# Logits with the masked keys of two heads as one stationary operand, in an attention and feed-forward kernel

## The chip, the cores and the metric

The kernel runs on one core of a Trainium2 chip. The metric is the device time of one execution in microseconds, as the median of several runs. The engines are called as in the profile: PE is the tensor engine and PEld its weight loads, DVE the vector engine, ACT the scalar engine, POOL the GpSimd engine, SP the engine that issues DMAs here. PSUM is the memory that PE writes; it has eight banks of 128 x 512 fp32.

## What is computed

A token gate mixes a segmented attention with a gated feed-forward network. Cut to what matters here:

```python
x = A_x                                        # (1, 2048, 512) bf16
g = sigmoid((x * gate_w).sum(-1, keepdims=True))
# attention: 32 heads of 16, four segments of 512 tokens
for s in range(4):
    logits = einsum('bhqd,bhkd->bhqk', qs, ks) * scale + mask   # causal within the segment
    p = softmax(logits); a_dot = p @ vs
    a_mem = (phi(qs) @ M) / (phi(qs) @ z + 1e-6)                # memory of the segments before
    o = sigmoid(beta) * a_mem + (1 - sigmoid(beta)) * a_dot
    M += phi(ks)^T @ vs; z += sum(phi(ks))
a = concat(o) @ wo
b = (relu(x @ W_gate) * (x @ W_up)) @ W_down   # inner width 1792
out = g * a + (1 - g) * b
```

## The kernel before

All weights and activations live on chip in bf16. The work is written as a list of named steps, about 1,100 of them, each with a function that emits its instructions on one engine, and with the steps that it depends on. A list of numbers, `ORDER`, gives for every engine the steps in the order in which that engine runs them, and on which engine a step with a choice runs. Each engine runs its own list strictly in that order, and waits where a dependency is not met. The numbers beside a step's engines are the plan's own costs; with a fixed `ORDER` they settle only which free PSUM bank a step gets.

Four PSUM banks, `rb`, go round among all dense matmul groups: a step takes a bank, and the step that copies the result out gives it back. The other four banks are one tile, `sp`, for the logits.

The dense steps, all on PE, go by segment (first digit) and a running number: `Q` and `K` project queries and keys, four 128-column chunks per segment, each four matmuls of 512 columns (line 477); `V` projects values (519, and `VI` at 502 for segment 0); `G` and `U` are the gate and up projections, 14 of each per segment (894); `D`, `DB` and `W` are the two halves of the down projection and the output projection that accumulates onto it (928, 941; for the last 128 rows in pieces at 852 and 860). `MR` retrieves from the memory (678), `MZ` updates it (632). Their results leave PSUM through `QC`, `KC`, `VC` (copies, 373 on ACT, 375 on DVE), `R` (ReLU, 906 on ACT, 908 on DVE), `H` (product, 913, DVE) and `OS` (scaling, 950 on ACT, 952 on DVE, and `ST` stores it).

One 128-row chunk of queries or keys holds eight heads of 16. It is read in four groups of 32 rows, two heads in each. The logits are made key by query, in blocks of 64 keys, and only where the causal mask lets them through: a block of keys `ck` sees the queries from `64*ck` on. A *part* is such a block with its columns of queries, 64 to 512 of them. Nine *fills* of `sp` take the parts of two chunks, each fill holding one part of 512 columns or two parts that make 512 together. So there are 72 fills: two pairs of chunks in four segments. `QK` (735) makes a fill, `EX` (746) takes the exponential of the whole of `sp` on ACT into one of nine `E` tiles, `MK` (756) zeroes the triangles on POOL, and `PV` (783) multiplies with the values after the fills of a chunk. The next fill must wait for `EX`, as there is one `sp`.

In `QK` each of the four row groups has two matmuls for a part. The even head's keys are the first 16 of the 32 rows, taken as they are with 16 rows of queries; for the odd head the step `KO` (490 on ACT, 492 on DVE) has made a copy of the keys, `KTo`, in which the even heads' rows are multiplied by zero (`mcol_o`), and the matmul uses all 32 rows. Each puts 64 keys in one half of the partitions of `sp`:

```python
for j, h in ((j, h) for j in range(4) for h in range(2)):
    kt = KTo[i] if h else KT[i]
    hi = 32 * j + 16 + 16 * h
    nc.tensor.matmul(sp[64 * h:64 * h + 64, j, off:off + m], ...)
```

`KT`, `KTo` and `QT` exist twice, for odd and even segments. The keys' copy `KT` also feeds the memory update: `EK` (608), `MN` (614), `PK` (618) and a transposing DMA `KX`. `MQ` and `MN` are clamps that run on DVE or POOL, and `TG` (565) is the product for the token gate in segment 0. On SP's queue stand the weight loads (324), the transposing load `XT` of a segment's x (336), `KX`, `MX`, the shifts of the values `VS` (450) and the stores. In the order of the last segment, PE ends with pieces for the last 128 rows of the output, 256, 128 and 128 columns wide.

Of the kernel before, what the change touches and what calls it, by code (L numbers as in the profile page):

```python
# [7 lines left out]
BF16 = mybir.dt.bfloat16  # L8
# [91 lines left out]
]  # L100
T0, TU, SPAN, PEN_D, PEN_A, PEN_P = 19.0, 15.6, 4.1, -23.0, 150.0, 146.0


PORT = {'TG', 'RN', 'RC', 'OA', 'KO', 'MB', 'MQ', 'MN', 'GS', 'PQ', 'PK', 'N1', 'N2', 'N3', 'NM'}
PIECE = {'MK': 0.445, 'TL': 0.22, 'ZE': 0.24, 'YL': 0.22, 'MB': 0.3}


# [898 lines left out]
```

## Time and profile before

| what | value |
|---|---|
| median of 3 runs | 266.98 us (266.53 to 267.01) |
| span of the profiled execution, first to last instruction | 265.0 us |
| instructions in it | 7943 |
| largest group on ACT | the exponential, 72 times, 135.1 us |
| largest group on POOL | the triangles, 256 instructions, 112.3 us |
| DVE's largest group | the product `H`, 56 times, 38.2 us |
| matmuls of `QK` | 1024, in 72 fills |
| HBM traffic | 8.26 MB read, 2.10 MB written |

The profiled execution has no other time of its own than its span; the runs' times include what lies around it. In the profile, a row of a group reads: line, engine, operation, what it writes and reads, shapes and count, then the busy time and the mean of one in ns, then the idle time of the engine before such instructions and what ended it. The chain of work that ended last is followed back from the last instruction. Matmuls are pipelined, so the length of one is not the pace of a row of them, and some of their records are missing.

### The profile page before, as it was taken

The page shows a single profiled execution, that of the slowest core. Times are in us where ns is not written, and L with a number is a line of the kernel's source. Part 1 is how long each engine was busy: PE and PEld are TensorE (multiplying, and loading weights), DVE is VectorE, ACT ScalarE, POOL GpSimd, SP SyncE. Part 2 cuts the span into 40 slices and gives each one's busy share as a digit, 9 for nine tenths or more (in the row PEclk, how much of TensorE's full clock was granted, in tenths as well). Part 3 has the DMA queues.
Part 4 walks back from the last instruction along what each step waited for, and adds up shares of the span by engine and source line. Part 5 has one row for each costly group of instructions (what it writes and reads, how often), then busy time and mean ns, then how long its engine had stood idle before and what let it go on. Part 6 is the DMA issues. An engine that isn't in the chain of part 4 may idle for free.

```text
span 265.0 us, 7943 instructions
## 1 busy us (share of the span) xinstructions
PE 258.1 (97%) x3293; PEld 121.0 (46%) x3337; DVE 181.0 (68%) x449; ACT 189.7 (72%) x185; POOL 143.7 (54%) x328
## 2 busy tenths in 40 slices
PE   7999999999999999999999999999999999999995
PEld 5444443545444444434444445454544444444554
DVE  1589788897774538855896476688878367666911
ACT  3699799987868786887777686886766576767012
POOL 8038978782826641378758464366468156064010
DMA  6978680426501000030403110000023100031002
GB/s 197 314 166 264 149 288 3 71 74 89 79 4 37 25 2 2 20 82 1 104 2 82 25 42 2 0 4 2 2 61 87 42 20 2 0 81 23 0 2 79
DMA packets 33422, 16.77 MB, mean 63 GB/s; under 512 B 20074, under 2 KB 33386, under 8 KB 33386
## 3 DMA queue, kind: packets, MB, share of 16 engines
q1 hardware_dynamic: 33098, 16.00, 24.3%
q8 instruction: 26, 0.43, 0.7%
q10 hardware_dynamic: 288, 0.26, 0.3%
q14 instruction: 10, 0.08, 0.1%
HBM read 8.26 MB, written 2.10 MB: 39 GB/s over the span
## 4 chain that ended last, share of the span: by engine, by line
PE 94%; DMA 1%; DVE 1%; issue 1%; ACT 1%; SPq 0%
PE rb L894 36%; PE rb L928 17%; PE rb L477 11%; PE sp L735 9%; PE rb L783 7%; PE rb L941 5%; PE rb L519 4%; DMA wv_sb<-in_A_wv_dram 1%; PE rb L678 1%; PE rb L852 1%; PE rb L502 1%; DVE hT L913 1%; ACT E L746 1%; PE rb L632 1%; PE rb L860 0%
## 5 line engine op out<-in xcount | busy, mean ns | idle before, releaser
L746 ACT ACTIVATE E<-sp 128x2048 bf16<-128x2048 f32 x72 | 135.1, 1877 | 35.0 <-PE sp L735 32.8
L756 POOL TENSOR_SCALAR_AFFINE_SELECT E<-E 64x256 bf16<-64x256 bf16 x256 | 112.3, 438 | 82.2 <-ACT E L746 68.7
L894 PE MATMUL rb<-xT,wg_sb 128*128 128x512 bf16 x216 | 55.4, 380 | 0.4
L894 PE MATMUL rb<-xT,wu_sb 128*128 128x512 bf16 x208 | 54.9, 380 | 0.8
L913 DVE TENSOR_TENSOR hT<-rb,rg 128x512 bf16<-128x512 f32 x56 | 38.2, 686 | 20.1 <-PE rb L894 14.1
L928 PE MATMUL rb<-wd_sb,hT 128*128 128x512 bf16 x198 | 48.6, 380 | 0.8 <-issue 0.2
L894 PEld LDWEIGHTS <-wg_sb 128*128 128x128 bf16 x224 | 20.7, 98 | 24.8 <-issue 3.1
L894 PEld LDWEIGHTS <-wu_sb 128*128 128x128 bf16 x224 | 20.1, 98 | 23.5 <-issue 4.5
L735 PE MATMUL sp<-QT,KT 16*64 16x320 bf16 (+7 forms) x512 | 30.3, 295 | 0.0
L735 PE MATMUL sp<-QT,KTo 32*64 32x320 bf16 (+7 forms) x512 | 30.3, 295 | 0.0
L928 PEld LDWEIGHTS <-hT 128*128 128x128 bf16 x210 | 19.4, 98 | 23.8 <-issue 3.2
L801 DVE STREAM_TRANSPOSE tA<-rb 128x512 f32<-128x512 f32 x32 | 21.9, 700 | 12.0 <-PE rb L783 11.6
L906 ACT ACTIVATE rg<-rb 128x512 bf16<-128x512 f32 x36 | 21.3, 598 | 10.1 <-PE rb L894 7.1
L735 PEld LDWEIGHTS <-KT 16*64 16x64 bf16 x512 | 10.5, 102 | 27.5 <-issue 26.9
L908 DVE TENSOR_SCALAR rg<-rb 128x512 bf16<-128x512 f32 x20 | 13.8, 688 | 7.5 <-PE rb L894 7.3
L783 PE MATMUL rb<-E,Vs 64*32 64x448 bf16 (+7 forms) x512 | 18.8, 284 | 0.0
L783 PE MATMUL rb<-E,Vp 64*32 64x448 bf16 (+7 forms) x512 | 18.4, 284 | 0.0
L950 ACT ACTIVATE osb<-rb,ngcol 128x512 bf16<-128x512 f32 x8 | 5.5, 691 | 16.2 <-PE rb L941 16.2
L952 DVE TENSOR_SCALAR osb<-rb,ngcol 128x512 bf16<-128x512 f32 x7 | 5.2, 750 | 16.1 <-PE rb L941 15.9
L477 PE MATMUL rb<-xT,wq_sb 128*128 128x512 bf16 x63 | 16.1, 380 | 0.0
L812 DVE TENSOR_TENSOR o<-tA,co 128x256 bf16<-128x256 f32 x32 | 15.4, 493 | 0.2
L477 PE MATMUL rb<-xT,wk_sb 128*128 128x512 bf16 x59 | 15.4, 379 | 0.2
(97 smaller groups left out, 298.3 us busy)
## 6 DMA issues: line engine op xcount, KB each, us to landing
out_dram<-osb SPq DMA_DIRECT2D x15, 128.0 KB, 1.8
wd_sb<-in_B_W_down_dram SPq DMA_DIRECT2D x1, 1792.0 KB
wg_sb<-in_B_W_gate_dram SPq DMA_DIRECT2D x3, 512.0 KB, 6.3
wu_sb<-in_B_W_up_dram SPq DMA_DIRECT2D x3, 512.0 KB, 6.0
Vs<-Vp SPq DMA_DIRECT2D x8, 144.0 KB, 3.2
wk_sb<-in_A_wk_dram SPq DMA_DIRECT2D x2, 256.0 KB, 3.9
wq_sb<-in_A_wq_dram SPq DMA_DIRECT2D x2, 256.0 KB, 4.7
wo_sb<-in_A_wo_dram SPq DMA_DIRECT2D x1, 512.0 KB, 4.2
```

What stands on the lines that cost most here:

```text
L477: nc.tensor.matmul(rb[s.bank][:], lhsT=w[:, ci, c * P:(c + 1) * P], rhs=xT[i][:, ci, :], start=(ci == 0), stop=(ci == NC - 1))
L735: nc.tensor.matmul(sp[64 * h:64 * h + 64, j, off:off + m], lhsT=kt[32 * j:hi, c0 + w, 64 * ck:64 * ck + 64], rhs=QT[i][32 * j:hi, c0 + w, ...
L746: nc.scalar.activation(Er[n % NE][:], sp[:], ACT.Exp, scale=SCALE)
L756: nc.gpsimd.affine_select(out=v, in_=v, compare_op=ALU.is_ge, fill=0.0, base=0, pattern=[[0, 4], [1, 64]], channel_multiplier=-1)
L783: nc.tensor.matmul(rb[s.banks[h]][32 * j:32 * j + 32, q0:q0 + m], lhsT=v[64 * h:64 * h + 64, ck // 2, o:o + 32], rhs=Er[(base + f) % NE][6 ...
L801: nc.vector.transpose(tA[k].rearrange("p b w -> p (b w)"), rb[a.banks[r]][:])
L812: nc.vector.tensor_tensor(o16[u % 2][:, :, r, :], tA[k][:, :, 0:DH], cos[k][:, :, None].to_broadcast([P, NB, DH]), ALU.mult)
L894: nc.tensor.matmul(rb[s.bank][:], lhsT=w[:, ci, fv * P:(fv + 1) * P], rhs=xT[i][:, ci, :], start=(ci == 0), stop=(ci == NC - 1))
L906: nc.scalar.activation(rgb[k][:], rb[a.bank][:], ACT.Relu)
L908: nc.vector.tensor_scalar(rgb[k][:], rb[a.bank][:], 0.0, None, ALU.max)
L913: nc.vector.tensor_tensor(hT[:, fv, :], rb[a.bank][:], rgb[k][:], ALU.mult)
L928: nc.tensor.matmul(rb[b][:], lhsT=hT[:, fv, lc:lc + P], rhs=wd_sb[:, fv, :], start=(fv == 0), stop=False)
```

## The change

For every segment and chunk the keys are now copied twice with a mask: `KO` for the odd heads, as before, and a new step `KE` for the even heads. Both copies go into one tile `KB`, in which each block of 64 keys has its even and odd copies next to each other, 128 columns. `QK` uses those as one stationary operand of 32 rows by 128 columns, with the 32 rows of queries, and writes all 128 partitions of a bank. `KB` exists once, not for odd and even segments, so both copies wait for the fills of the segment before that read the same chunk; the waits of `QC` and `KC` are split to match. In the last two segments the two parts of a fill are made in reverse order. The plan's cost of a fill goes from 0.262 to 0.236. `ORDER` is another list, for 1129 steps in place of 1113, with other places and other engines for many steps.

```diff
-    mcol_o = sb([1], F32, "mcol_o")
+    mcol = [sb([1], F32, f"mcol{r}") for r in range(2)]
...
-    nc.vector.memset(mcol_o[:], 1.0)
-    for j in range(4):
-        nc.vector.memset(mcol_o[32 * j:32 * j + 16, :], 0.0)
+    for r in range(2):
+        nc.vector.memset(mcol[r][:], 1.0 * r)
+        for j in range(4):
+            nc.vector.memset(mcol[r][32 * j:32 * j + 16, :], 1.0 - r)
...
-    KTo = [sb([NC, L], BF16, f"KTo{i}") for i in range(2)]
+    KB = sb([NC, L // 64, 2, 64], BF16, "KB")
...
-                prev = [] if not old else old["qk"][c] + old.get("kr", [])
+                if what == "Q":
+                    prev = old["qk"][c] if old else []
+                else:
+                    prev = old["KO"][2 * c:2 * c + 2] + old.get("kr", [])[c:c + 1] if old else []
...
-            def ko(e, s, c=c):
-                if e == "ACT":
-                    nc.scalar.activation(KTo[i][:, c, :], KT[i][:, c, :], ACT.Copy, scale=mcol_o[:, 0:1])
-                else:
-                    nc.vector.tensor_scalar(KTo[i][:, c, :], KT[i][:, c, :], mcol_o[:, 0:1], None, ALU.mult)
-            d["KO"].append(add(f"KO{seg}{c}", {"DVE": 0.27, "ACT": (0.62, 60.0)}, ko, after=[d["K"][c]], prio=want))
+            for r, kind in ((1, "KO"), (0, "KE")):
+                def ko(e, s, c=c, r=r):
+                    o, k = KB[:, c, :, r, :], KT[i][:, c, :].rearrange("p (k q) -> p k q", q=64)
+                    if e == "ACT":
+                        nc.scalar.activation(o, k, ACT.Copy, scale=mcol[r][:, 0:1])
+                    else:
+                        nc.vector.tensor_scalar(o, k, mcol[r][:, 0:1], None, ALU.mult)
+                d["KO"].append(add(f"{kind}{seg}{c}", {"DVE": 0.27, "ACT": (0.62, 60.0)}, ko,
+                                   after=[d["K"][c]] + (st[seg - 1]["qk"][c] if seg else []), prio=want))
...
-                for _, w, m, ck, q0, off in whole[f]:
-                    for j, h in ((j, h) for j in range(4) for h in range(2)):
-                        kt = KTo[i] if h else KT[i]
-                        hi = 32 * j + 16 + 16 * h
-                        nc.tensor.matmul(sp[64 * h:64 * h + 64, j, off:off + m],
-                                         lhsT=kt[32 * j:hi, c0 + w, 64 * ck:64 * ck + 64],
-                                         rhs=QT[i][32 * j:hi, c0 + w, q0:q0 + m],
-                                         start=True, stop=True, tile_position=(32 * j, 64 * h))
-            a = add(f"QK{seg}{c0}{f}", {"PE": 0.262}, qk, mode="rows",
-                    after=[x for w in us for x in (d["Q"][c0 + w], d["KO"][c0 + w], d["K"][c0 + w])] + fills[-1:],
+                for _, w, m, ck, q0, off in (reversed(whole[f]) if seg > 1 else whole[f]):
+                    for j in range(4):
+                        js = slice(32 * j, 32 * j + 32)
+                        nc.tensor.matmul(sp[:, j, off:off + m],
+                                         lhsT=KB[js, c0 + w, ck].rearrange("p r k -> p (r k)"),
+                                         rhs=QT[i][js, c0 + w, q0:q0 + m],
+                                         start=True, stop=True, tile_position=(32 * j, 0))
+            a = add(f"QK{seg}{c0}{f}", {"PE": 0.236}, qk, mode="rows",
+                    after=[x for w in us for x in [d["Q"][c0 + w], *d["KO"][2 * (c0 + w):2 * (c0 + w) + 2]]] + fills[-1:],
                     prio=tu - 20.0, lat=0.25)
```

Some of the new order, by the steps' names. PE around the first fill of segment 1: `QK028 MR15 D03 D00 QK100` (before `QK028 D00 MR14 MZ1 QK100`). ACT there: `EX028 KE13 KO13 EX100` (before `EX028 EX100`). PE's last steps: `D31 D33 W30 DB33 W32 DB31 D33 W31 W33 DB33 W33` (before `D31 DB30 D33 D32 DB32 DB31 W30 DB33 W31 W32 D33 DB33 W33 D33 W33 DB33 W33`). SP's first: gate and up pieces 0, 1 and 2, then `XT1` (before pieces 0, gate 1 and up 2, then `XT1`).

More of the change, by code (lines that the diff above doesn't have):

```diff
@@ L41 @@
 ORDER = [
[58 rows of a table removed]
[61 rows of a table added]
 ]
 T0, TU, SPAN, PEN_D, PEN_A, PEN_P = 19.0, 15.6, 4.1, -23.0, 150.0, 146.0
-PORT = {'TG', 'RN', 'RC', 'OA', 'KO', 'MB', 'MQ', 'MN', 'GS', 'PQ', 'PK', 'N1', 'N2', 'N3', 'NM'}
+PORT = {'TG', 'RN', 'RC', 'OA', 'KO', 'KE', 'MB', 'MQ', 'MN', 'GS', 'PQ', 'PK', 'N1', 'N2', 'N3', 'NM'}
 PIECE = {'MK': 0.445, 'TL': 0.22, 'ZE': 0.24, 'YL': 0.22, 'MB': 0.3}
```

119 rows, old and new, of the table ORDER are left out of this document.

## The prediction

> **What bounds the kernel now.** I read the page first: the busy times, the forty slices and the chain that ended last.
>
> ```profile
> span 265.0 us, 7943 instructions
> PE 258.1 (97%) x3293; PEld 121.0 (46%) x3337; DVE 181.0 (68%) x449; ACT 189.7 (72%) x185; POOL 143.7 (54%) x328
> PE   7999999999999999999999999999999999999995
> PE 94%; DMA 1%; DVE 1%; issue 1%; ACT 1%; SPq 0%
> PE rb L894 36%; PE rb L928 17%; PE rb L477 11%; PE sp L735 9%; PE rb L783 7%; PE rb L941 5%; PE rb L519 4%; DMA wv_sb<-in_A_wv_dram 1%; PE rb L678 1%; PE rb L852 1%; PE rb L502 1%; DVE hT L913 1%; ACT E L746 1%; PE rb L632 1%; PE rb L860 0%
> ```
>
> TensorE carries 94% of the chain and is in the nines from the second slice to the last but one. A busy PE need not be a full one, so I looked at where its matmuls start in the chain and in the timeline. The x8 pieces of the chain give 1.73 us for eight dense matmuls of 512 columns, 0.216 each. Walking the matmul starts from 7.3 us to the end, every step is either this pitch, a change of shape, or a hole of exactly one pitch. The holes are lost records: the page has 3293 matmuls for 3337 weight loads. So PE has no real wait between 7.3 and 262 us, and its work turns into span one for one. Everything else matters only if it makes PE wait.
>
> **What a fill of logits costs on PE.** The timeline of PE around one fill (start, length, what), a piece of the chain, and the groups by shape (busy, mean ns):
>
> ```profile
> 41.41 1.73 PE rb L894 x8
> ...
> 108.78 1.89 PE L894 MATMUL rb<-xT,wg_sb 128*128 128x512 bf16 x8
> 110.60 0.40 PE L735 MATMUL sp<-QT,KT 16*64 16x512 bf16 x1
> ...
> 110.62 0.40 PE L735 MATMUL sp<-QT,KTo 32*64 32x512 bf16 x1
> 110.95 0.39 PE L894 MATMUL rb<-xT,wg_sb 128*128 128x512 bf16 x1
> ...
> L894 PE MATMUL rb<-xT,wg_sb 128*128 128x512 bf16 x216 | 55.4, 380 | 0.4
> L735 PE MATMUL sp<-QT,KT 16*64 16x512 bf16 x64 | 6.7, 398 | 0.0
> L735 PE MATMUL sp<-QT,KT 16*64 16x448 bf16 x64 | 5.9, 351 | 0.0
> ```
>
> The eight dense matmuls end their streaming at 108.78 + 1.73 = 110.51. The next dense matmul starts at 110.95. The fill takes 0.44 us here; in ns over all fills I read 448, whether it has 8 matmuls (one part of 512 columns) or 16 (two parts that add up to 512). It splits so. (1) About 93 ns from the end of dense streaming to the first start. (2) A load that the first part waits for: the 512-column matmul lasts 398 and the 448-column one, always a second part, 351; 64 columns of streaming are 27 ns, so some 20 to 25 remain. (3) 213 ns of streaming. (4) A stagger of seven steps of 3.3 ns, 110.60 to 110.62: 23 ns. (5) About 93 ns until dense work starts. The sum is 93 + 25 + 213 + 23 + 93 = 447.
>
> **The change, part by part.** *Half the matmuls.* A part becomes 4 instructions, one for each 32 rows, instead of 8. Streaming is unchanged, since the rows already worked side by side. The stagger falls to three steps, 10 ns: 13 ns gained. *The stationary operand* grows from 64 to 128 columns. What the first part then waits for isn't in this trace for 32 rows. The nearest row is the dense operand of 128 columns: the dense matmul right behind a fill lasts 0.39 against a mean of 380 ns, some 11 ns of exposed load; the 64-column load costs 25. Ends: 11 ns (as dense) and 50 ns (twice the 64-column one). Records of the loads themselves do not separate them:
>
> ```profile
> L894 PEld LDWEIGHTS <-wg_sb 128*128 128x128 bf16 x224 | 20.7, 98 | 24.8 <-issue 3.1
> L735 PEld LDWEIGHTS <-KT 16*64 16x64 bf16 x512 | 10.5, 102 | 27.5 <-issue 26.9
> ```
>
> I take 11: the new operand has the dense one's width and is contiguous. The fill becomes 93 + 11 + 213 + 10 + 93 = 420, a gain of 27 ns; 72 fills give **1.94 us**. At the other end it is 459, a loss of 12 ns and 0.9 us in all. Taking the parts of a fill in reverse in the last two segments changes none of these terms.
>
> [...]
>
> *Sixteen more masking steps.* Even keys, read until now as 16 unmasked rows, get their own masked copy. The new order puts 10 of them on DVE and 6 on ACT, and splits the odd ones 10 and 6 (before 11 and 5). Rows for one copy:
>
> ```profile
> L492 DVE TENSOR_SCALAR KTo<-KT,mcol_o x11: 313/347/551, 10.8 to 181.9; 128x512 bf16<-128x512 bf16 x11
> L490 ACT ACTIVATE KTo<-KT,mcol_o x5: 712/712/712, 22.0 to 221.2; 128x512 bf16<-128x512 bf16 x5
> ```
>
> That is 9 x 0.347 = 3.1 us more on DVE and 7 x 0.712 = 5.0 on ACT. The output now lies in runs of 64, which the trace does not show; between 0.31 and the 0.69 of DVE's plain copies out of PSUM I take 0.347, since the operand and its type are the same. The cover is DVE's and ACT's idle time (84 and 75 us by the page), but not evenly: see the rivals.
>
> *One copy of the masked keys.* The masking of a segment now waits until the fills of the segment before have read the same columns. The tightest place in the order is ACT, where both copies of chunk 3 stand between the last exponential of segment 0 and the first of segment 1: 2 x 0.712 = 1.4 us. Queued behind them is that exponential, and behind it the next fill. PE has a retrieval piece and two down-projection halves (0.18 + 2 x 1.51 = 3.2 us) before the fill that the exponential waits for, so the 1.4 us lie under PE's work; without that cover they would cost at most 1.4.
>
> *The order anew.* I counted its steps by engine. PE does the same work with the same number of mode changes (164 between neighbours). From R (ReLU) 12 steps move from ACT to DVE, of K and V copies 7, and DVE gets 3 more clamps of POOL's. By rows of 0.69, 0.41 to 0.69 and 0.32 us this is some 17 us more on DVE in all, 198 of 263, and 8 less on ACT: neither is a bound over the whole span. On SP two weight loads of 512 KB now stand before the transposing load of the second segment's x. At 319 GB/s in that stretch they hold it up by 3 us; its first user stands one fill (about 3 us) later than before.
>
> ```profile
> 0.00:7.30 7.30, 5.74 (x42) 3.81 (x43) 1.78 (x11) 2.84 (x6) 5.31 (x13) 1.00 0.68 208
> 7.30:14.00 6.70, 6.65 (x35) 3.10 (x33) 3.53 (x10) 4.15 (x10) 0.00 (x0) 1.00 0.99 319
> 14.00:25.00 11.00, 10.89 (x111) 4.82 (x118) 9.77 (x26) 10.63 (x13) 6.79 (x12) 1.00 0.85 223
> 14.00:63.20 49.20, 48.67 (x700) 22.74 (x707) 41.63 (x101) 44.91 (x48) 36.04 (x78) 1.00 0.52 134
> ```
>
> These are busy us of PE, PE's loads, DVE, ACT, POOL, then the granted clock (1.00 throughout), the DMA share and GB/s. The start up to 7.3 us is held by the first loads, which stay; its matmuls are only permuted, so I put it at 0, within 0.2 either way. *The end:* the last full output tile is now finished just before the last small one.
>
> ```profile
> 258.77 0.75 DVE L952 TENSOR_SCALAR osb<-rb,ngcol 128x512 bf16<-128x512 f32 x1 [6.29 <-PE rb L941]
> 262.08 0.35 DVE L871 TENSOR_SCALAR rg<-rb,ngcol 128x128 bf16<-128x128 f32 x1 [2.56 <-PE rb L860]
> ...
> 261.40 1.43 SPq L877 DMA_DIRECT2D out_dram<-rg  x2
> ```
>
> Its 0.75 on DVE lies under the three small PE pieces that follow (about 0.83), and its store goes out shortly before the last one: 0 to 0.3 us, I take 0.1. *Small waits of PE* in the first stage (below) I put at 0.3, from ends of 0 and 2.6.
>
> **The sum.** 265.0 - 1.94 + 0.1 + 0.3 = 263.5 us of span. The runs' median is 266.98, so 1.9 to 2.0 lie around the profiled span; with that the time is **265.4 us**. The fills' own range with start and end is 264.6 to 266.2.
>
> **The rivals.**
>
> *DVE and ACT bind the first stage (slower).* Between the first and the last fill of segment 0 (14.0 to 63.2) DVE and ACT are busy 86.5 of 98.4 us, and in its first 11 us ACT stands at 97%. By the new order's steps there (five copies of even keys and one of odd keys more, two R, three clamps and two token-gate products more, some two and a half retrieval groups less) DVE gets about 5.0 more and ACT 0.3: 91.8 of 99.2, DVE at 94%. The four banks then come back late, and PE, which runs in order, waits for them. If the two engines need the idle share they had (12%), the stage takes 91.8 / 0.879 / 2 = 52.2 instead of 49.6: 2.6 us lost, less the 1.94, gives 267.7. It decides against the change from 1.94 us of waits on. For it: those shares. Against it: before, the first 11 us ran at 93% of both engines without one wait of PE. Strided copies at 0.69 would feed it with up to 2 us.
>
> *The load is not faster (slower).* With 50 ns exposed the fills lose 0.9 us: 268.2 with the waits above. For it, the 25 ns of the present tiles; against it, the 11 of dense ones.
>
> *The loads of the four row groups follow each other instead of overlapping (no change).* Two dense loads in a row start 15 ns apart; three such steps, 45 ns in place of 10, give 455 a fill, +0.5 us, or with half of it hidden the old 448: 267.0 to 267.9. That would also be the outcome if the matmul count did not matter.
>
> **How the numbers follow.** The forecast has 0.62, a variant of it that gains more at start or end (264.3) 0.02, the first stage 0.20 (a third of it ending near 267.0, the rest at 267.7), the slow load 0.06, the loads in a row 0.08 (mostly no change), and other waits of the new order 0.02. About 0.2%, 0.5 us, is what can be told from no change: faster 0.64, same 0.12, slower 0.24. The range for 8 in 10 runs from 264.4 to 267.8; the forecast's own is 264.6 to 266.2.
>
> **What would show it.** The fills: dense to dense across a fill near 0.42 us, four starts some 3 ns apart, the 512-column matmul near 385 instead of 398. If it stays at 398 or grows to 425, the load step is wrong; if starts lie 15 ns apart, the loads follow each other. The first stage: PE gaps between 14 and 63 us that are no lost records, ended by DVE's or ACT's copies. The masking copies: DVE at 0.35, ACT at 0.71. The exponential after the last of segment 0 should find its fill done just before. The forecast is wrong if the fills gain 27 ns and the span does not fall by over a microsecond.

## The result and the profile after

The changed kernel takes 269.86 us (269.76 to 270.09) against 267.00 us before: 1.0105 times as long, with an interval of 1.0092 to 1.0118. The profiled span is 268.2 us. Forecast were 265.4 us and a range of 264.4 to 267.8, so the sign was wrong. The experiments below are compared with the kernel before as it ran beside them: 267.24 us beside the first four experiments, 266.97 beside the last.

The page of the changed kernel: span, busy times, the slices of PE and of its clock, the queues that carry instructions, and the chain.

```profile
span 268.2 us, 6946 instructions
PE 257.9 (96%) x2789; PEld 118.8 (44%) x2825; DVE 194.3 (72%) x486; ACT 184.5 (69%) x170; POOL 143.7 (54%) x327
PE   7999969999999999999999999999999999999995
PEclk9999997999999999999999999999999999999999
q8 instruction: 22, 0.36, 0.6%
PE 93%; issue 2%; DVE 2%; DMA 1%; SPq 1%
```

Two things are new: a 6 in PE's sixth slice (33.5 to 40.2 us of the span), and a row for the clock, which was not on the page before, with a 7 in the next slice. The chain holds 2% of "issue", time in which the engine waited for nothing that the profile shows.

The fills did what was forecast. Their groups by shape (columns: busy, mean ns of one | idle time before):

```profile
L744 PE MATMUL sp<-QT,KB 32*128 32x512 bf16 x64 | 6.3, 385 | 0.0
L744 PEld LDWEIGHTS <-KB 32*128 32x128 bf16 x512 | 8.3, 92 | 29.9 <-issue 28.6 <-DVE memT L575 0.4 <-ACT e1k L618 0.4
```

PE's timeline around one of them (start, length, instruction):

```profile
44.14 0.38 PE L481 MATMUL rb<-xT,wq_sb 128*128 128x512 bf16 x1
44.45 0.40 PE L744 MATMUL sp<-QT,KB 32*128 32x512 bf16 x4
44.78 0.39 PE L903 MATMUL rb<-xT,wu_sb 128*128 128x512 bf16 x1
```

The last dense matmul starts at 44.14 and streams until 44.36; dense work goes on at 44.78. That is 0.42 us for the fill; over the fills I read 423 ns where there were 448. The 512-column matmul fell from 398 to 385 ns.

Now PE's timeline from 37.1 us; the bracket holds the idle time before a row:

```profile
36.92 0.33 PE L642 MATMUL rb<-Vp,pK 128*32 128x34 bf16 x17
37.19 0.39 PE L744 MATMUL sp<-QT,KB 32*128 32x192 bf16 x6
40.02 0.45 PE L744 MATMUL sp<-QT,KB 32*128 32x320 bf16 x2 [2.44 <-issue]
40.40 0.61 PE L903 MATMUL rb<-xT,wg_sb 128*128 128x512 bf16 x1
```

The windows of the changed kernel around it (length, then busy us of PE, its loads, DVE, ACT and POOL, the granted clock, DMA share with 1 for all sixteen engines, GB/s; the times of packets overlap, so the share can read above 1):

```profile
31.00:37.40 6.40, 6.35 (x168) 3.07 (x167) 4.46 (x12) 6.25 (x9) 3.15 (x9) 1.00 1.08 343
37.40:40.00 2.60, 0.18 (x6) 0.00 (x0) 1.30 (x5) 0.34 (x1) 2.40 (x6) 0.96 0.46 84
40.00:43.20 3.20, 2.96 (x8) 1.14 (x10) 0.88 (x3) 2.48 (x2) 1.43 (x5) 0.50 0.02 5
```

PE stops in the middle of a fill, after six of its eight matmuls, for 2.44 us. The last two read the same tiles as the six before them, which had already run, and no other engine is late: DVE, ACT and then POOL run dry behind PE. From 39.8 to 43.2 us the granted clock is 0.50, and the dense matmuls there start 0.43 us apart instead of 0.216.

What was moving at that time was not PE's data but its instructions. The DMA queues of the changed kernel from 33.4 to 37.3 us, and from 37.3 to 38.7:

```profile
DMA packets 1344, 1.36 MB, mean 349 GB/s; under 512 B 16, under 2 KB 1344, under 8 KB 1344
q1 hardware_dynamic: 1344, 1.36, 109.5%
...
DMA packets 456, 0.20 MB, mean 144 GB/s; under 512 B 360, under 2 KB 455, under 8 KB 455
q1 hardware_dynamic: 455, 0.19, 54.3%
q8 instruction: 1, 0.02, 5.0%
```

The first two rows are 33.4 to 37.3 us: all sixteen engines full with the weight loads, and no packet of the instruction queue. The others are 37.3 to 38.7: one instruction packet of 16 KB, which starts at 37.41, as the loads drain (their last packets start near 37.7), and ends at 38.53. PE goes on 1.5 us later. The loads are those of `W_down` and `wo`. SP's own timeline shows them in the changed kernel:

```profile
28.47 0.57 SPq L328 DMA_DIRECT2D wd_sb<-in_B_W_down_dram  x1
29.10 1.79 SPq L328 DMA_DIRECT2D wo_sb<-in_A_wo_dram  x1
```

and in the kernel before:

```profile
32.87 0.57 SPq L324 DMA_DIRECT2D wd_sb<-in_B_W_down_dram  x1
...
50.31 0.58 SPq L324 DMA_DIRECT2D wo_sb<-in_A_wo_dram  x1
```

The page of before has the row of the instruction queue too:

```profile
q8 instruction: 26, 0.43, 0.7%
```

That is 22 packets for the 5,650 loads and matmuls that PE runs now (2825 loads, each with its matmul), and 26 for the 6,674 of before: one for every 257 of them, in both kernels. I take a packet as a block of 256 instructions. Laid against PE's program, a packet is then due when PE is about 177 + 256n instructions along. This place is a fit: from the sixth block on, in all kernels of this study, the fetch starts between 2.4 us before it and 1.9 us after it. In the changed kernel PE stops some 270 instructions after the block was due (behind its 351st load, at 702 instructions, where the block was due at 433), and I take that as the point by which PE must have it.

The block in question, in all kernels of this study. Times in us, read from the trace's single records; the columns are when PE comes to instruction 433 (by the fit, the block falls due), when it comes to 689, the fetch, and PE's idle time in the pause.

| kernel | at 433 | at 689 | fetch | pause |
|---|---|---|---|---|
| before | 28.79 | 36.54 | 28.61 to 30.25 | none |
| after | 33.36 | 37.05 | 37.41 to 38.53 | 2.44 |
| first experiment: both loads late | 33.38 | 37.08 | 34.81 to 35.74 | none |
| second: `wo` late | 33.11 | 36.80 | 36.80 to 37.94 | 2.01 |
| third: 26 instructions fewer ahead | 34.01 | 38.77 | 38.17 to 39.30 | 0.28 |
| fourth: old order | 34.00 | 45.40 | 37.31 to 38.44 | none |
| fifth: start | 33.19 | 36.88 | 34.11 to 35.09 | none |

In the changed kernel two things met. The fetch came 4.0 us after it was due. And PE goes through these 256 instructions in 3.7 us, where before it took 7.8. Of their 128 matmuls, 29 were dense before, beside the 64 of the first `PV` and 35 of `QK`. The new order has put `MZ` there: 63 of its matmuls, 49 of `PV` and 8 of `QK` leave room for 8 dense ones. Neither alone makes a pause: the kernel before goes through another 256 instructions in 3.7 us as well (62.05 to 65.76), with a fetch that starts 1.1 us after it is due, and in the fourth experiment below the fetch starts 3.3 us late, but PE takes 11.4 us.

In all three kernels that pause, the pause stands at the same count, behind PE's 351st weight load, in whatever step that falls, and ends 1.4 to 1.5 us after the fetch.

### The profile page after: what moved, and what is told of

It is laid out like the page before. It is cut to its first block, busy times and chain, and to the rows that moved or that the text cites. A ratio compares the mean times of both kernels' runs of the same rounds, so it can differ in the third digit from the quotient of the medians.

```text
span 268.2 us, 6946 instructions
## 1 busy us (share of the span) xinstructions
PE 257.9 (96%) x2789; PEld 118.8 (44%) x2825; DVE 194.3 (72%) x486; ACT 184.5 (69%) x170; POOL 143.7 (54%) x327
## 4 chain that ended last, share of the span: by engine, by line
PE 93%; issue 2%; DVE 2%; DMA 1%; SPq 1%
PE rb L903 37%; PE rb L937 17%; PE rb L481 10%; PE sp L744 9%; PE rb L792 7%; PE rb L950 5%; PE rb L529 4%; DMA xT<-in_A_x_dram 1%; PE rb L688 1%; PE rb L861 1%; PE rb L512 1%; SPq L349 1%; PE rb L642 1%; PE rb L869 0%; DVE QT L379 0%
## 5 line engine op out<-in xcount | busy, mean ns | idle before, releaser
L765 POOL TENSOR_SCALAR_AFFINE_SELECT E<-E 64x256 bf16<-64x256 bf16 x256 | 114.9, 449 | 101.4 <-ACT E L755 88.7
L903 PE MATMUL rb<-xT,wg_sb 128*128 128x512 bf16 x218 | 56.6, 383 | 0.5 <-issue 0.2
L922 DVE TENSOR_TENSOR hT<-rb,rg 128x512 bf16<-128x512 f32 x56 | 37.7, 680 | 7.6 <-PE rb L903 3.9
L744 PE MATMUL sp<-QT,KB 32*128 32x320 bf16 (+6 forms) x512 | 29.0, 287 | 2.7 <-issue 2.4
L917 DVE TENSOR_SCALAR rg<-rb 128x512 bf16<-128x512 f32 x32 | 21.8, 683 | 9.1 <-PE rb L903 8.8
L744 PEld LDWEIGHTS <-KB 32*128 32x128 bf16 x512 | 8.3, 92 | 29.9 <-issue 28.6
L915 ACT ACTIVATE rg<-rb 128x512 bf16<-128x512 f32 x24 | 14.1, 598 | 6.8 <-PE rb L903 4.7
L961 DVE TENSOR_SCALAR osb<-rb,ngcol 128x512 bf16<-128x512 f32 x9 | 6.6, 744 | 15.3 <-PE rb L950 15.3
L950 PE MATMUL rb<-wo_sb,oT 128*128 128x512 bf16 x57 | 14.8, 379 | 0.4 <-issue 0.3
L529 PE MATMUL rb<-wv_sb,xT 128*128 128x257 bf16 (+1 forms) x96 | 14.5, 273 | 0.0
L821 DVE TENSOR_TENSOR o<-tA,co 128x256 bf16<-128x256 f32 x32 | 14.1, 466 | 0.0
```

Of the source, the lines that this page charges most:

```text
L529: nc.tensor.matmul(rb[s.bank][:, 0:n], lhsT=xT[i][:, ci, t * P:(t + 1) * P], rhs=wv_sb[:, ci, h * D // 2:h * D // 2 + n], start=(ci == 0), ...
L744: nc.tensor.matmul(sp[:, j, off:off + m], lhsT=KB[js, c0 + w, ck].rearrange("p r k -> p (r k)"), rhs=QT[i][js, c0 + w, q0:q0 + m], start=T ...
L765: nc.gpsimd.affine_select(out=v, in_=v, compare_op=ALU.is_ge, fill=0.0, base=0, pattern=[[0, 4], [1, 64]], channel_multiplier=-1)
L903: nc.tensor.matmul(rb[s.bank][:], lhsT=w[:, ci, fv * P:(fv + 1) * P], rhs=xT[i][:, ci, :], start=(ci == 0), stop=(ci == NC - 1))
L917: nc.vector.tensor_scalar(rgb[k][:], rb[a.bank][:], 0.0, None, ALU.max)
L922: nc.vector.tensor_tensor(hT[:, fv, :], rb[a.bank][:], rgb[k][:], ALU.mult)
```

## The experiments

**Both loads late.** The changed kernel with the loads of `W_down` and `wo` (129 and 134 in `ORDER`) behind the first transposing DMA `KX` of segment 1 on SP.

```diff
+def late(steps, behind):
+    for v in steps:
+        ORDER.remove(v)
+    at = ORDER.index(behind) + 1
+    ORDER[at:at] = steps
+late([129, 134], 2464)
```

> The changed kernel; on SP the loads of W_down and wo (2.3 MB) are issued behind the first transposing DMA of segment 1 (about 37 us) instead of ahead of it (28.5 and 29.1). Fetch theory: PE's pause of 2.44 us inside a fill at 37.6 us is a block of 16 KB of its own instructions that came late, behind these loads, and the halved clock that follows is due to the pause. Then the block is fetched near 33.5 instead of 37.4, there is no pause and no halved clock, and the kernel gains 2.4 to 2.9 us for the pause and about 1.6 for the clock: near 265.5 us. Rival, the new order binds PE through its banks: the pause stays, near 269.9. Rival, the pause belongs to the new matmul form: it stays.

Measured: 265.72 us, 0.9944 of before (0.9923 to 0.9966). Its window over the first stage (columns as above):

```profile
14.00:63.20 49.20, 49.12 (x573) 21.71 (x571) 44.68 (x108) 44.68 (x46) 35.57 (x83) 1.00 0.66 141
```

and PE's timeline at the fill in question:

```profile
36.60 0.68 PE L652 MATMUL rb<-Vp,pK 128*32 128x34 bf16 x64
37.22 0.40 PE L754 MATMUL sp<-QT,KB 32*128 32x192 bf16 x8
37.55 1.04 PE L913 MATMUL rb<-xT,wg_sb 128*128 128x512 bf16 x4
```

All eight matmuls run through, the clock stays at 1.00, and PE is busy 49.12 of 49.20 us. Only one real wait of PE is left in that stage, 0.14 us up to 22.84, where a weight load waits for the second segment's x:

```profile
22.84 0.33 PEld L491 LDWEIGHTS <-wk_sb 128*128 128x128 bf16 x3 [0.35 <-DMA xT<-in_A_x_dram]
```

The fetch came at 34.81, 1.4 us after it was due; I had expected 33.5. It is the only packet of its time, as the DMA queues from 34.7 to 35.8 us show:

```profile
DMA packets 1, 0.02 MB, mean 15 GB/s; under 512 B 0, under 2 KB 0, under 8 KB 0
q8 instruction: 1, 0.02, 5.3%
```

So about 1.4 of the 4.0 us are there without the loads. PE comes to its 352nd load at 37.23, 1.5 us after the end of the fetch, so the deadline is met here with next to nothing to spare. The pause belongs neither to the new matmul form nor to DVE and ACT giving banks back late: the form and the order of every engine but SP are as in the changed kernel.

**Only `wo` late.** The same with `late([134], 2464)`.

> The changed kernel; only the load of wo (0.5 MB) is issued behind the first transposing DMA of segment 1. Fetch theory: the backlog ahead of PE's block is 0.5 MB shorter, 1.5 us at about 0.35 MB per us; the block starts near 35.9 instead of 37.4 and is there by 37.1, just before PE needs it at 37.6: the pause is under 0.5 us, and the time between 265.4 and 266.5. If the clock falls only after a long pause it stays whole. Rivals (banks, form of the matmul): the pause stays at 2.4 us, near 269.9.

Measured: 267.62 us, 1.0014 (0.9992 to 1.0035). A miss in size: the fetch moved by 0.6 us, not by 1.5, as `W_down` alone kept the engines busy until 36.8, and the pause stayed:

```profile
36.94 0.39 PE L754 MATMUL sp<-QT,KB 32*128 32x192 bf16 x6
39.34 0.31 PE L754 MATMUL sp<-QT,KB 32*128 32x320 bf16 x2 [2.01 <-issue]
39.58 0.60 PE L913 MATMUL rb<-xT,wg_sb 128*128 128x512 bf16 x2
```

But it separates the pause from the clock. In the profiled execution the clock stayed at 1.00 after a pause of 2.0 us. Of ten runs two had a mean clock of 0.994, the value of the changed kernel's runs, and took 268.9 us; the other eight, at 0.999 to 1.000, took 267.3 on average. The halved clock thus costs 1.6 us. The first experiment's time lies 1.6 us below the eight, and 2.0 below the profiled one of them, whose pause is 2.01: that is the pause. How long it was in the other nine is not on record.

**Fewer instructions ahead.** The changed kernel, loads untouched; the warm-up at the start uses 6 matmuls of 400 columns instead of 19 of 128, so PE has 13 loads and 13 matmuls fewer to run.

```diff
-NWARM = 19
+NWARM = 6
...
-    zeros = sb([P], BF16, "zeros")
+    zeros = sb([400], BF16, "zeros")
...
-                nc.tensor.matmul(rb[3][:, 0:P], lhsT=zeros[:], rhs=zeros[:], start=True, stop=True)
+                nc.tensor.matmul(rb[3][:, 0:400], lhsT=zeros[:, 0:P], rhs=zeros[:], start=True, stop=True)
```

> The changed kernel with its loads where they are; the 19 warm-up matmuls of 128 columns are 6 of 400, so that 26 instructions fewer stand ahead of everything. Fetch theory: the loads hold the block until 37.4 as before, but PE reaches the end of the instructions that it has 26 instructions later, some 2.3 us of dense work; the pause shrinks to under 0.7 us, and the time falls to between 265.5 and 267. A rival by which PE's position in the code does not matter (banks, an operand, the form of the matmul) leaves the pause at the same fill and at 2.4 us, near 269.9.

Measured: 266.17 us, 0.9960 (0.9945 to 0.9975). The fetch is as late as before (38.17), but PE needs the block later, and the pause shrinks to 0.28 us, at another place of the program: between two matmuls of a query projection at 40.3, not in the fill.

```profile
39.20 0.81 PE L903 MATMUL rb<-xT,wu_sb 128*128 128x512 bf16 x3
39.84 1.31 PE L481 MATMUL rb<-xT,wq_sb 128*128 128x512 bf16 x4
41.09 0.40 PE L744 MATMUL sp<-QT,KB 32*128 32x512 bf16 x4
```

Four matmuls take 1.31 us there instead of 1.03. The place is 13 matmuls further on, as many as were taken out ahead. This run also has a wait of 0.58 us up to 23.41, where the first experiment has 0.14: a projection waits for the second segment's x and for a bank, which come within 0.06 us of each other; why they come later here is not shown. That wait and the pause make 0.72 of the 0.8 us between the two profiled spans (264.8 and 264.0). No load and no order had been changed; that the pause follows the count of instructions shows what it is.

**The new operand in the old order.** `ORDER` of the kernel before; each `KE` right behind its `KO` on the same engine; the rest as changed.

```diff
+        had = [s for s in self.steps if s.name[:2] != "KE"]
         for v in ORDER:
-            queues[ENGINES[v % len(ENGINES)]].append(self.steps[v // len(ENGINES)])
+            s = had[v // len(ENGINES)]
+            queues[ENGINES[v % len(ENGINES)]] += [s, self.steps[s.seq + 1]] if s.name[:2] == "KO" else [s]
```

> The new operand alone: the order of the kernel before, with each even-key copy put right behind the odd one on the same engine; one copy of the masked keys, as in the changed kernel. In this order the second block of instructions is used up only about 11 us after it is begun, so the fetch theory expects no pause, and 72 fills at 0.423 instead of 0.448 us: 1.8 us less than before, less what the 16 copies cost the first stage: 265.2 to 266.2. The rival that I had forecast (DVE and ACT bind the first stage) expects waits of PE between 14 and 63 us that eat the gain: 267 or more.

Measured: 266.02 us, 0.9956 (0.9941 to 0.9971). No pause: `MZ` stands ten microseconds later in this order, and the block lasts until 45.4. The new operand by itself is a gain. And the interval overlaps that of the first experiment, so a gain by the new order itself is not shown. PE has five small waits here (at 24.8, 41.9, 81.8, 95.0 and 113.2 us), 0.9 us in all, which the order before did not have with fewer copies. One row among the groups of this run shows where a part is from: the masking copies now wait for fills, since there is only one `KB`.

```profile
L500 DVE TENSOR_SCALAR KB<-KT,mcol 128x512 bf16<-128x512 bf16 x22 | 8.3, 418 | 2.5 <-PE sp L743 1.8 <-ACT KT L376 0.7
```

**The start.** The first experiment's kernel, with the third tile of x transposed ahead of the fourth on PE.

```diff
+late([180, 190, 210, 200], 410)
```

> The kernel of the first experiment (W_down and wo late), and PE transposes the third tile of x ahead of the fourth at the start, behind the value matmuls of the first two tiles, as the kernel before does. Theory of the start: in the changed order PE waits 0.72 us at 6.4 us for the fourth tile of x, which lands last, while the third is there; with the tiles in the order of landing its waits up to 8.3 us fall from 3.2 to about 2.6 us, and the time by 0.4 to 0.7 from 265.7 to near 265.2. Rival: the start is bound by the loads whatever is transposed first; then nothing changes, 265.7.

Measured: 265.89 us, 0.9965 (0.9951 to 0.9978), and waits of PE of 3.1 us up to 8.3 us, as in the first experiment (3.2). No gain. PE then waits for a copy on ACT that frees a bank instead of the tile:

```profile
4.49 2.54 PE L523 MATMUL rb<-wv_sb,xT 128*128 128x512 bf16 x8
6.88 0.52 PE L405 MATMUL rb<-ident,xT 128*128 128x128 bf16 x6
7.61 0.27 PE L405 MATMUL rb<-ident,xT 128*128 128x128 bf16 x2 [0.22 <-ACT xT L388]
```

My theory of the start falls. The fourth experiment, with the old start, has 2.4 us of such waits; why the new start needs 0.6 more is left open.

## Why the prediction was wrong, step by step

**The fills** were right. Forecast were 27 ns less, 1.94 us in all; measured are 448 - 423 = 25 ns, 1.8 us. The stagger fell to 10 ns as said. The 128-column operand exposes a load near the dense one's and not twice the 64-column one's, which the 385 ns of the 512-column matmul show: 13 ns less than the 398 of before, as forecast. So the rivals of a slow load and of loads in a row fell. The 213 ns of streaming that the forecast's sum uses agree with rows of the kernel before in which only the columns differ: the matmuls of `PV` last 376 ns for 512 columns and 296 for 320, which makes 0.417 a column.

**The masking copies** were right: medians of 344 ns on DVE (forecast 347; the mean is 395) and 712 on ACT, strided output or not. **The chunk-3 copies** between two segments delayed nothing on PE.

**DVE and ACT in the first stage**, the slower rival, was not it. With the loads moved, the same order runs that stage with DVE and ACT at 91% each (forecast 94 and 92) and 0.14 us of waits of PE. I had put 0.3 there. That wait is not for DVE or ACT but for the transposing load of x, which lands at 22.8 us instead of 19.5: the delay of 3 us that the prediction took as covered by a later first user.

**The end** was right: 3.2 us from the last matmul's start to the end, before and after. **The start** was off: waits up to 8.3 us rose from 2.6 to 3.2 us, where I had allowed 0.2.

**The step that failed** is "The order anew", where I went through SP's queue. I counted the two loads that now stand before the transposing load of x and asked who waits for that transfer. I did not go on to the next two, `W_down` and `wo`, which the new order issues at 28.5 and 29.1 us instead of 32.9 and 50.3, and I took it that only transfers wait for transfers. PE's own instructions come over the DMA engines too (the 22 packets of q8, of 16 KB each), and behind these loads their block came 4.0 us after it was due and cost PE the pause and the clock. The page of before showed them (q8, 26 packets) and I read past that row. In the kernel before, the next block after this one was fetched at 39.27, behind `W_down`, 2.7 us after it was due, and PE, by the count of 270, needed it only 6.6 us after the fetch had ended; that was the warning.

The rest of the account for the profiled spans, after less before: the pause 2.7 us (the fill's seventh matmul starts that much after its sixth; the profile's 2.44 count from the sixth one's end), the halved clock 1.5 (from the seventh to the next fill 4.43 us, where the first experiment takes 2.93), the wait for x 0.1, the start 0.6, and the fills 1.8 less; together 3.1, against 268.2 - 265.0 = 3.2. Without pause and clock, as in the first experiment, the time is 265.7 us, within 0.3 of the forecast. So the span met the sign of failure that the prediction had set itself, fills 25 ns shorter and no shorter span, and not by way of a rival that it had named.

So part of the verdict on the change is a verdict on where two loads stand. With these two moved it beats the kernel before by 0.6% (0.9944, 0.9923 to 0.9966), the lowest ratio of this study, though the intervals of the last three experiments overlap with it.

## What to carry to other kernels

In this kernel, where PE runs nearly without a gap, its instruction stream was one more input with a deadline: a block whose fetch started 4.0 us after it was due cost a pause of 2.44 us. Look at the instruction packets on the page, find the stretches in which 256 instructions go by quickly (here 3.7 us, with 120 of 128 matmuls small tiled ones), and keep large loads from filling the DMA queues just before them; with both loads moved, the fetch here started 1.4 us after it was due, and there was no pause. The number of instructions ahead counts as well: 26 fewer at the start moved the pause 13 matmuls on and took it from 2.44 to 0.28 us. A pause marked "issue" in the middle of a group of matmuls that needs nothing new was the sign of it here.

## What the runs showed of the hardware that was not expected

A fetch of 16 KB took 0.9 to 1.6 us of DMA time, and behind the loads of `W_down` and `wo` it started 3.7 to 4.2 us after it was due (the changed kernel, the second and the third experiment), with the engines all but idle 1.4 (the first); PE went on 1.4 to 1.5 us after its end (40.02 after 38.53, 39.34 after 37.94, 40.77 after 39.30).

The clock was halved for 3.4 us, from 39.8 to 43.2, in the changed kernel's trace, with a pause of 2.4 us before it. Its four runs all have the mean clock of 0.994 that this gives. Of the ten runs of the second experiment two have it; the one that was profiled has 1.00 after a pause of 2.0. What sets the clock down in some runs and not in others is not shown.
